# A concatenated kernel of dilated attention and a state-space scan: projections reordered, logits partly summed on TensorE, states stacked, and three engines in a written order

## The chip, the cores and the metric

The kernel runs on one core of one Trainium2 chip. A core has a matrix engine (PE, TensorE), a vector engine (DVE), a scalar engine (ACT), GpSimd (POOL) and a queue engine (SP) that issues DMAs. The metric is the device time of one execution in microseconds; lower is better. A trace by the hardware profiler accompanies it.

## The reference

Two independent parts read the same kind of input and are concatenated along the last axis. S = 2048 positions, D = 448 features, bf16 in and out.

```python
# A: sliding dilated attention, 16 heads of 28, window of 8 positions 2 apart
qkv = x @ wqkv                       # split into q, k, v per head
idx = pos[:, None] - 2 * arange(8)   # earlier positions only, masked where negative
logits = einsum("bhsd,bhswd->bhsw", q, k[idx]) * 28 ** -0.5
o = einsum("bhsw,bhswd->bhsd", softmax(logits), v[idx])
a = o @ wo
# B: diagonal complex state space, P = 448 states
Lam_bar = exp(exp(log_dt) * Lam);  B_bar = ((Lam_bar - 1) / Lam)[:, None] * Bmat
h_t = Lam_bar * h_{t-1} + B_bar @ x_t           # over 2048 steps
y = 2 * real(h @ Cmat.T) + x * Dskip
return concatenate([a, y], -1)
```

## The kernel before

**Part A.** A partition holds 16 consecutive positions (J = 16). `g_xta` transposes x on PE, four blocks of 128x112 into one PSUM tile, and DVE copies that to `xTA`. `proj(t, ...)` (L144 matmuls, L146 ACT copies) then computes v, k and q, in this order, sixteen positions of four matmuls of 448 columns each. The 14 positions before a partition's first one, the halo, come from the partition below: four DMAs on SP per tensor (L149 to L152) copy them inside SBUF. The one of L151 starts at partition 112, which the one of L150 writes too; the one of L152 fills a lone row. For each of the 8 offsets w DVE multiplies q by the shifted k (L327, `pr`, 7168 elements per partition), then adds halves (L329, L330) and, for two offsets together, the rest of a tree (L331 to L333) to give the logits `L`. Softmax runs on DVE with one Exp on ACT (L341). Then DVE multiplies the weights by v (L380, `pv`), PE sums over the 8 offsets and transposes at once by matmuls with the identity into `acc` (L385), ACT copies `acc` to `oT` (L387), and `wo_group` multiplies by wo (L367) and stores `ya`.

**Part B.** Time is cut into 512 chunks of T = 4 steps. x is transposed on PE (`g_x4`, L116) into `xT4`; B likewise (`g_bt`, L110, copied by ACT at L111) and C (`g_ct`, L122). The 448 states have a real and an imaginary tile of 112 rows for each of four `pt`: eight tiles. For each step j, Bu takes four matmuls (L256), and from j = 1 two more with diagonal matrices `dg` that carry the state of the step before (L260, L261). `ssm_chunk_scan` on DVE rotates by the tables `tab` (cos, sin), scans over the 512 chunks (L278) and rotates back, for each half of the tiles. A fix (L294 to L296) adds the chunk's incoming state to steps 0 to 2, and `c_side` (L306, L308) multiplies by C and the skip term and stores `yo`. Parameters (powers of Lam_bar, `dg`, C's weights `Cw`, the tables) are computed on DVE and ACT from four vectors of 448 numbers.

**What sets the order.** The program is written in the order v, small parameters, k, Cw, q, B's transposes, Bu, scans, fix, C, logits, softmax, output. A list scheduler of the framework reorders each engine's instructions; semaphores keep the dependences. Each engine runs its own list in order. A DMA is issued by the engine on whose queue it stands (SP, ACT or POOL), which waits there for what the DMA needs; DMA semaphores are reused in turn, so that an issue can also wait for an earlier DMA that used the same one.

Of the kernel before, what the change touches and what calls it, by code (L numbers as in the profile page):

```python
# [8 lines left out]
BF16 = mybir.dt.bfloat16  # L9
# [10 lines left out]
T = 4  # L20
NC = S // T
# [6 lines left out]
def kernel(  # L28
# [21 lines left out]
    const = ctx.enter_context(tc.tile_pool(name="const", bufs=1))  # L50
    psum = ctx.enter_context(tc.tile_pool(name="ps", bufs=4, space=bass.MemoryType.PSUM))
    pst_ctx = ExitStack()
    psum_t = pst_ctx.enter_context(tc.tile_pool(name="pst", bufs=2, space=bass.MemoryType.PSUM))
    ident = const.tile([128, 128], BF16, tag="ident")
    make_identity(nc, ident[:])

    bk = ctx.enter_context(tc.tile_pool(name="b_keep", bufs=1, side="right"))
    bx = ctx.enter_context(tc.tile_pool(name="b_x", bufs=1, side="right"))
    bn_ctx = ExitStack()
    bn = bn_ctx.enter_context(tc.tile_pool(name="b_n", bufs=1, side="right"))  # L60
    ak = ctx.enter_context(tc.tile_pool(name="a_keep", bufs=1))
    qk_ctx = ExitStack()
    qkp = qk_ctx.enter_context(tc.tile_pool(name="a_qk", bufs=1))
    ain_ctx = ExitStack()
    ain = ain_ctx.enter_context(tc.tile_pool(name="a_in", bufs=1))

    def rows112(src):
        return src.rearrange("(k p) n -> p k n", p=KT)
    xnA = ain.tile([128, J, D], BF16, tag="xnA")
    xA_r = A_x[0].rearrange("(p j) d -> p j d", j=J)  # L70
    nc.sync.dma_start(xnA[:, 0:4, :], xA_r[:, 0:4, :])
    nc.sync.dma_start(xnA[:, 4:8, :], xA_r[:, 4:8, :])
    nc.sync.dma_start(xnA[:, 8:12, :], xA_r[:, 8:12, :])
    nc.sync.dma_start(xnA[:, 12:16, :], xA_r[:, 12:16, :])
    wq = ain.tile([KT, 4, 3 * D], BF16, tag="wqkv")
    nc.sync.dma_start(wq[:, 0:2], rows112(A_wqkv)[:, 0:2])
    nc.sync.dma_start(wq[:, 2:4], rows112(A_wqkv)[:, 2:4])

    raws = []
    for i, (vec, name) in enumerate(((B_Lambda_re, "lre"), (B_Lambda_im, "lim"), (B_log_dt, "ld"), (B_Dskip, "dsk"))):  # L80
        raw = const.tile([KT, 4], BF16, tag=name + "_raw", name=name + "_raw")
        nc.sync.dma_start(raw[:], vec.rearrange("(t i) -> i t", i=KT))
        raws.append(raw)
    Cn = bn.tile([KT, 2, 4, D], BF16, tag="Cn")
    nc.sync.dma_start(Cn[:, 0], rows112(B_C_re))
    nc.gpsimd.dma_start(Cn[:, 1], rows112(B_C_im))
    Bn = bn.tile([KT, 2, 4, D], BF16, tag="Bn")
    nc.sync.dma_start(Bn[:, 0], rows112(B_B_re))
    nc.gpsimd.dma_start(Bn[:, 1], rows112(B_B_im))
    xnB = bx.tile([128, 4, T, D], BF16, tag="xnB")  # L90
    xB_r = B_x[0].rearrange("(cb p j) d -> p cb j d", p=128, j=T)
    nc.sync.dma_start(xnB[:, 0:2], xB_r[:, 0:2])
    nc.gpsimd.dma_start(xnB[:, 2:4], xB_r[:, 2:4])

    xTA = ain.tile([KT, 4, J, 128], BF16, tag="xTA")
    CT = bn.tile([KT, 4, 2, D], BF16, tag="CT")
    BT = bk.tile([KT, 4, 2 * D], BF16, tag="BT")
    xT4 = bk.tile([KT, 4, T, NC], BF16, tag="xT4")
    idk = ident[0:KT, 0:KT]

    def g_xta(jg, kt):
        tp = psum_t.tile([128, 4, 128], BF16, tag="tp", name="tp")
        for jj in range(4):
            PE.transpose(tp[0:KT, jj, :], xnA[:, 4 * jg + jj, KT * kt:KT * (kt + 1)], ident[:])  # L104
        V.tensor_copy(xTA[:, kt, 4 * jg:4 * jg + 4, :], tp[0:KT])  # L105

    def g_bt(ri, kt):
        tp = psum_t.tile([128, 4, 128], BF16, tag="tp", name="tp")
        for pt in range(4):
            PE.transpose(tp[0:KT, pt, 0:KT], Bn[:, ri, pt, KT * kt:KT * (kt + 1)], idk)  # L110
        ACT.copy(BT[:, kt, ri * D:(ri + 1) * D].rearrange("p (a b) -> p a b", a=4), tp[0:KT, :, 0:KT])  # L111

    def g_x4(kt, j):
        tp = psum_t.tile([128, 4, 128], BF16, tag="tp", name="tp")
        for cb in range(4):
            PE.transpose(tp[0:KT, cb, :], xnB[:, cb, j, KT * kt:KT * (kt + 1)], ident[:])  # L116
        ACT.copy(xT4[:, kt, j, :], tp[0:KT])

    def g_ct(ri, pt):
        tp = psum_t.tile([128, 4, 128], BF16, tag="tp", name="tp")  # L120
        for dtile in range(4):
            PE.transpose(tp[0:KT, dtile, 0:KT], Cn[:, ri, dtile, KT * pt:KT * (pt + 1)], idk)  # L122
        V.tensor_copy(CT[:, pt, ri, :].rearrange("p (a b) -> p a b", a=4), tp[0:KT, :, 0:KT])

    groups = ([(g_xta, (jg, kt)) for jg in range(4) for kt in range(4)]
              + [(g_ct, (ri, pt)) for ri in range(2) for pt in range(4)]
              + [(g_bt, (ri, kt)) for ri in range(2) for kt in range(4)]
              + [(g_x4, (kt, j)) for j in range(T) for kt in range(4)])

    def next_group(n=1, late=False):  # L130
        for _ in range(n):
            if groups and (late or groups[0][0] in (g_xta, g_ct)):
                fn, args = groups.pop(0)
                fn(*args)
    next_group(4)

    q_s = qkp.tile([128, DH, J, H], BF16, tag="q_s")
    k_s = qkp.tile([128, JK, DH, H], BF16, tag="k_s")
    v_s = ak.tile([128, JK, DH, H], BF16, tag="v_s")
    def proj(t, dst, joff):  # L140
        for j in range(J):
            ps = psum.tile([128, 512], F32, tag="mm")
            for kt in range(4):
                PE.matmul(ps[:, 0:D], xTA[:, kt, j, :], wq[:, kt, t * D:(t + 1) * D], start=(kt == 0), stop=(kt == 3))  # L144
            o_ap = dst[:, :, j, :] if t == 0 else dst[:, joff + j, :, :]
            ACT.copy(o_ap, ps[:, 0:D].rearrange("p (h d) -> p d h", h=H))  # L146
            next_group()
        if t != 0:
            nc.sync.dma_start(dst[1:65, 0:HALO], dst[0:64, J:JK])  # L149
            nc.sync.dma_start(dst[65:113, 0:HALO], dst[64:112, J:JK])  # L150
            nc.sync.dma_start(dst[112:128, 0:HALO], dst[111:127, J:JK])  # L151
            nc.sync.dma_start(dst[0:1, 0:HALO], dst[0:1, J:JK])  # L152

    proj(2, v_s, HALO)
    def pt_(name):
        return const.tile([KT, 4], F32, tag=name, name=name)
    lre, lim, ld, dsk = [pt_(n) for n in ("lre", "lim", "ld", "dsk")]
    for f_, r_ in zip((lre, lim, ld, dsk), raws):
        V.tensor_copy(f_[:], r_[:])
    hpib = const.tile([KT, 1], F32, tag="hpib")  # L160
    nc.gpsimd.memset(hpib[:], 0.5 * PI * SHR)
# [9 lines left out]
    def sincos(sin_out, cos_out, y, kM, pool, shape, tagp):  # L171
        nfr = pool.tile(shape, F32, tag=tagp + "nfr", name=tagp + "nfr")
        V.scalar_tensor_tensor(nfr[:], kM, -MAGIC, y, ALU.add, ALU.subtract)
        ACT.activation(sin_out, nfr[:], ACTF.Sin, scale=-2 * PI * SHR)
        afr = pool.tile(shape, F32, tag=tagp + "afr", name=tagp + "afr")
        ACT.activation(afr[:], nfr[:], ACTF.Abs)
        ACT.activation(cos_out, afr[:], ACTF.Sin, bias=hpib[:], scale=-2 * PI * SHR)

    dt = pt_("dt"); ACT.activation(dt[:], ld[:], ACTF.Exp)
    are = tt(pt_("are"), dt, lre, ALU.mult)  # L180
    th = tt(pt_("th"), dt, lim, ALU.mult)
    r = pt_("r"); ACT.activation(r[:], are[:], ACTF.Exp)
    rT = pt_("rT"); ACT.activation(rT[:], are[:], ACTF.Exp, scale=float(T))
    f = ts(pt_("f"), th, 1.0 / (2 * PI), ALU.mult)
    fT = ts(pt_("fT"), th, float(T) / (2 * PI), ALU.mult)
    kM1 = pt_("kM1"); V.tensor_scalar(kM1[:], f[:], 1.0, MAGIC, ALU.mult, ALU.add)
    sn = pt_("sn"); cs = pt_("cs")
    sincos(sn[:], cs[:], f[:], kM1[:], const, [KT, 4], "p_")
    pwall = const.tile([KT, T - 1, 3, 4], F32, tag="pwall")
    a1 = tt(pwall[:, 0, 0, :], r, cs, ALU.mult)  # L190
    b1 = tt(pwall[:, 0, 1, :], r, sn, ALU.mult)
    pw = [(a1, b1)]
    t0 = pt_("t0"); t1 = pt_("t1")
    for k in range(2, T):
        ap, bp = pw[-1]
        ak_ = pwall[:, k - 1, 0, :]; bk_ = pwall[:, k - 1, 1, :]
        tt(ak_, ap, a1, ALU.mult); tt(t0, bp, b1, ALU.mult); tt(ak_, ak_, t0, ALU.subtract)
        tt(bk_, ap, b1, ALU.mult); tt(t0, bp, a1, ALU.mult); tt(bk_, bk_, t0, ALU.add)
        pw.append((ak_, bk_))
# [25 lines left out]

    proj(1, k_s, HALO)
    Cw = bk.tile([KT, 8, D], BF16, tag="Cw")
    dgD = bk.tile([KT, 4, KT], BF16, tag="dgD")
    for pt in range(4):
        c1 = slice(pt, pt + 1)  # L230
        tmp = bn.tile([KT, D], F32, tag="ctmp")
# [189 lines left out]
```

## Time and profile before

| | |
|---|---|
| median of 3 runs | 231.79 us (231.47 to 232.53) |
| span of the profiled execution | 227.3 us, 3441 instructions; 4.5 us less than the median |
| PE, weight loads | 181.1 us (80%), 118.0 us (52%) |
| DVE | 161.9 us (71%) |
| ACT | 105.1 us (46%) |
| mean granted TensorE clock | 0.946 |
| read from HBM, written | 6.88 MB, 3.67 MB |

The time of the profiled execution itself is not listed beside its span, so the difference between median and span, 4.5 us, is taken for what lies around the span. Busy times are of one profiled execution. An engine's slices are 40 equal parts of the span, each digit the busy share in tenths. The chain of waits is the work that ended last, followed back from the end at each step to what released it. A group's line reads: line of the kernel, engine, operation, out<-in, shapes, count | busy us, mean ns of one | idle time before them and what ended most of it. Matmuls are pipelined, so the mean of one is longer than the distance from one start to the next.

### The profile page before, as it was taken

To read this page: it belongs to the slowest core of one execution; us is meant where nothing else is said; L and a number is where in the kernel's file an instruction comes from. 1 tells how busy PE (TensorE), PEld (TensorE's weight loads), DVE (VectorE), ACT (ScalarE), POOL (GpSimd) and SP (SyncE) were. 2 spreads that over 40 slices of the span, in tenths; PEclk is the share of its full clock that TensorE was granted. 3 is DMA by queue.
4 is the path that set the end of the run, shared out by engine and by line. 5 is a ranking of instruction groups with operands and counts; after the bars stand their busy time and mean duration, and the time that the engine had idled before them with its cause. 6 is when DMAs were issued, how large, how long until landed. Compare 5 with 4: busy or idle time off the path is not lost.

```text
span 227.3 us, 3441 instructions
## 1 busy us (share of the span) xinstructions
PE 181.1 (80%) x1400; PEld 118.0 (52%) x1400; DVE 161.9 (71%) x200; ACT 105.1 (46%) x186; POOL 4.8 (2%) x18
## 2 busy tenths in 40 slices
PE   2008995989997999999969400599999996999993
PEld 2004662645555666566536200255555696887961
DVE  1103779794007999179999999999867999999022
ACT  2001691898678876454438300293345213234151
POOL 6000000000000000000000000000000000000000
PEclk9999999799999799999999955599999999999999
DMA  6999300392752000000000000001112230020213
GB/s 227 283 291 204 136 4 0 71 178 40 141 108 35 3 0 0 3 0 0 0 0 0 3 0 0 0 0 40 62 43 81 62 114 3 0 84 3 82 36 128
DMA packets 9996, 14.02 MB, mean 62 GB/s; under 512 B 2716, under 2 KB 8188, under 8 KB 9724
## 3 DMA queue, kind: packets, MB, share of 16 engines
q1 hardware_dynamic: 9612, 12.07, 21.2%
q0 software_dynamic: 368, 1.72, 2.6%
q8 instruction: 11, 0.18, 0.3%
q14 instruction: 5, 0.04, 0.1%
HBM read 6.88 MB, written 3.67 MB: 46 GB/s over the span
## 4 chain that ended last, share of the span: by engine, by line
PE 57%; DVE 25%; ACT 8%; DMA 7%; SPq 1%; issue 1%
PE acc L385 13%; PE ps L144 12%; PE ps L306 11%; DMA wq<-in_A_wqkv_dram 7%; PE psf L256 6%; PE ps L367 5%; DVE pr L327 5%; DVE scr L278 4%; DVE pr L329 3%; DVE dg L212 2%; PE tp L116 2%; PE psf L295 2%; PE psf L296 1%; PE ps L308 1%; PE psf L261 1%; PE psf L260 1%
## 5 line engine op out<-in xcount | busy, mean ns | idle before, releaser
L144 PE MATMUL ps<-wq,xTA 112*128 112x448 bf16 x192 | 44.9, 376 | 15.6 <-DMA wq<-in_A_wqkv_dram 11.9
L327 DVE TENSOR_TENSOR pr<-q_s,k_s 128x7168 bf16<-128x7168 bf16 x8 | 31.1, 3885 | 15.9 <-ACT q_s L146 15.9
L256 PE MATMUL psf<-xT_115,BT 112*112 112x512 bf16 x128 | 33.7, 386 | 0.0
L380 DVE TENSOR_TENSOR pv<-attn,v_s 128x1792 bf16<-128x1792 bf16 x32 | 32.2, 1082 | 0.0
L385 PE MATMUL acc<-ident,pv 128*112 128x128 bf16 x512 | 29.2, 219 | 2.0 <-ACT oT L387 2.0
L385 PEld LDWEIGHTS <-pv 128*112 128x112 bf16 x512 | 29.0, 130 | 2.3 <-issue 2.0
L144 PEld LDWEIGHTS <-xTA 112*128 112x128 bf16 x192 | 18.9, 103 | 20.3 <-issue 4.3
L306 PE MATMUL ps<-Cw,Z 112*128 112x448 bf16 x128 | 26.8, 352 | 0.0
L262 ACT CAST Z<-psf 112x512 bf16<-112x512 f32 x32 | 18.8, 587 | 16.9 <-PE psf L261 15.5
L295 PE MATMUL psf<-Z,dg 112*112 112x511 bf16 x24 | 10.1, 419 | 18.8 <-DVE Z L282 18.8
L297 ACT CAST Z<-psf 112x512 bf16<-112x512 f32 x24 | 14.0, 585 | 22.9 <-PE psf L296 21.7
L256 PEld LDWEIGHTS <-BT 112*112 112x112 bf16 x128 | 16.7, 132 | 9.9
L146 ACT CAST v_s<-ps 128x448 bf16<-128x448 f32 x16 | 8.3, 538 | 26.8 <-PE ps L144 26.7
L105 DVE COPY xTA<-tp 112x512 bf16<-112x512 bf16 x16 | 6.7, 422 | 19.6 <-PE tp L104 19.4
L387 ACT CAST oT<-acc 112x2048 bf16<-112x2048 f32 x4 | 7.5, 1865 | 22.8 <-PE acc L385 22.8
L310 ACT CAST yo<-ps 128x448 bf16<-128x448 f32 x16 | 8.3, 531 | 17.9 <-DMA out_dram<-yo 9.8
L104 PEld LDWEIGHTS <-xnA 128*112 128x112 bf16 x64 | 7.3, 164 | 18.0 <-issue 12.5
L306 PEld LDWEIGHTS <-Z 112*128 112x128 bf16 x128 | 11.8, 98 | 9.0
L329 DVE TENSOR_TENSOR pr<-pr 128x3584 bf16<-128x3584 bf16 x8 | 16.1, 2016 | 0.1
L296 PEld LDWEIGHTS <-dg 112*112 112x112 bf16 x24 | 3.4, 142 | 21.5 <-issue 19.9
L367 PE MATMUL ps<-wo_p,oT 112*128 112x448 bf16 x64 | 12.6, 352 | 0.0
L104 PE MATMUL tp<-ident,xnA 128*112 128x128 bf16 x64 | 7.7, 259 | 4.4 <-DMA xnA<-in_A_x_dram 4.3
(131 smaller groups left out, 234.3 us busy)
## 6 DMA issues: line engine op xcount, KB each, us to landing
xnA<-in_A_x_dram SPq DMA_DIRECT2D x4, 448.0 KB, 6.8
out_dram<-yo SPq DMA_DIRECT2D x16, 112.0 KB, 1.7
out_dram<-ya SPq DMA_DIRECT2D x16, 112.0 KB, 1.7
wq<-in_A_wqkv_dram SPq DMA_DIRECT2D x2, 588.0 KB
xnB<-in_B_x_dram POOLq DMA_DIRECT2D x1, 896.0 KB, 13.2
xnB<-in_B_x_dram SPq DMA_DIRECT2D x1, 896.0 KB
v_s<-v_s SPq DMA_DIRECT2D x1, 784.0 KB
k_s<-k_s SPq DMA_DIRECT2D x1, 784.0 KB
```

The costliest lines, as they stand in the source:

```text
L104: PE.transpose(tp[0:KT, jj, :], xnA[:, 4 * jg + jj, KT * kt:KT * (kt + 1)], ident[:])
L144: PE.matmul(ps[:, 0:D], xTA[:, kt, j, :], wq[:, kt, t * D:(t + 1) * D], start=(kt == 0), stop=(kt == 3))
L256: PE.matmul(ps[:], BT[:, kt, ri * D + KT * pt: ri * D + KT * (pt + 1)], xT4[:, kt, j, :], start=(kt == 0), stop=(kt == 3 and j == 0))
L262: ACT.copy(Z[:, ri * 4 + pt, j, :], ps[:])
L295: PE.matmul(ps[:, 1:NC], dg[:, pt, j, ia, :], Z[:, pt, T - 1, 0:NC - 1], start=False, stop=False)
L297: ACT.copy(Z[:, ri * 4 + pt, j, :], ps[:])
L306: PE.matmul(ps[:, 0:D], Z[:, k8, j, cols], Cw[:, k8, :], start=(k8 == 0), stop=False)
L327: V.tensor_tensor(pr.rearrange("p d (j h) -> p d j h", h=H), q_s[:], k_s[:, off:off + J].rearrange("p j d h -> p d j h"), ALU.mult)
L329: V.tensor_tensor(pr[:, 0:14, :], pr[:, 0:14, :], pr[:, 14:28, :], ALU.add)
L367: PE.matmul(ps[:, 0:D], oT[:, kt, j, :], wo_p[:, kt, :], start=(kt == 0), stop=(kt == 3))
L380: V.tensor_tensor(pv[:], attn[:, w, JG * H * jg:JG * H * (jg + 1)].rearrange("p (j h) -> p j h", h=H) .unsqueeze(2).to_broadcast((128, JG, ...
L385: PE.matmul(acc[0:KT, kt, jj, :], pvf[:, jj, KT * kt:KT * (kt + 1)], ident[:], start=(w == 0 and jj == 0), stop=(w == W - 1 and jj == JG - 1))
```

## The change

- **Order of part A.** The projections are now k, q, v. x is loaded in four pieces with k's weights second; weights are loaded per projection. k's halo DMAs are issued from ACT, v's from SP.
- **Logits.** Each offset is cut in two halves of 8 positions. DVE multiplies and adds the two halves of the head dimension once; PE sums the remaining 14 terms in PSUM by matmuls with the identity; ACT copies the result to `L`.
- **States.** Seven tiles of 128 rows, each 64 real rows above the same 64 imaginary ones. One matrix `R` of 128x128 per tile and power carries the complex product, in place of two diagonal ones. The scan's rotation reads rows 0 to 63 and writes rows 64 to 127, and the reverse.
- **B's x** is transposed by eight DMAs on SP, straight to `xT4`. B's and C's loads move from POOL to SP. The vectors come in twelve small DMAs on POOL into 33 rows, ahead of the identity on POOL, and are transposed on PE. Tables are computed once in natural order and spread to the stacked order by twelve DMAs on SP. C is interleaved by POOL.
- **Written order.** From v's projection on, PE, DVE and ACT run in the order in which the program emits them. `fill(us)` takes pieces of PE work from a list until their written cost reaches the given time; `qk_unit` places such a piece between the DVE work of a unit and its matmuls. After unit 12 the list holds three pieces, so the loop `while len(work) > 12` takes none; the scans of both halves follow unit 12, and units 13 to 15 come after them.

```diff
+    for hj in range(2):
+        xh = qkp.tile([128, 8, D], BF16, tag="prod", bufs=3, name="xh")
+        nc.sync.dma_start(xh[:, 0:4], xA_r[:, 8 * hj:8 * hj + 4])
+        if hj == 0:
+            load_w(1)
+        nc.sync.dma_start(xh[:, 4:8], xA_r[:, 8 * hj + 4:8 * hj + 8])
+    load_w(0)
...
+    for j in range(T):
+        nc.sync.dma_start_transpose(xT4[:, 0:3, j, :], xB_r[j, :, 0:384])
+        nc.sync.dma_start_transpose(xT4[:, 3, j, :], xB_r[j, :, 320:448])
+    rows = const.tile([33, 128], BF16, tag="rows")
+    for r0, vec in ((0, B_Lambda_re), (7, B_Lambda_im), (18, B_log_dt)):
+        for hf in range(2):
+            nc.gpsimd.dma_start(rows[r0:r0 + 7, 64 * hf:64 * hf + 64], vec.rearrange("(m i) -> m i", i=64))
...
     ident = const.tile([128, 128], BF16, tag="ident")
     make_identity(nc, ident[:])
...
+    for jg in range(4):
+        for kt in range(4):
+            g_xta(jg, kt)
+        for j in range(4 * jg, 4 * jg + 4):
+            proj_j(1, k_s, HALO, j)
+    halo(nc.scalar, k_s)
...
+    for j in range(J):
+        proj_j(0, q_s, 0, j)
+    ctx.enter_context(tc.manual_schedule(engines={nc.tensor.engine, nc.vector.engine, nc.scalar.engine}))
...
+    def qk_unit(u, us):
...
+        V.tensor_tensor(pr.rearrange("p d (j h) -> p d j h", h=H), q_s[:, :, 8 * jh:8 * jh + 8, :],
+                        k_s[:, off + 8 * jh:off + 8 * jh + 8].rearrange("p j d h -> p d j h"), ALU.mult)
+        V.tensor_tensor(pr[:, 0:14, :], pr[:, 0:14, :], pr[:, 14:28, :], ALU.add)
+        fill(us)
+        for d in range(14):
+            PE.matmul(lgs[g][:, wi, 128 * jh:128 * jh + 128], ident[:], pr[:, d, :], start=(d == 0), stop=(d == 13))
+        if u % 4 == 3:
+            ACT.copy(L[:, 2 * g:2 * g + 2, :], lgs[g][:])
...
+    for u in range(13):
+        qk_unit(u, 2.3)
+    while len(work) > 12:
+        fill(0.1)
+    ssm_chunk_scan(HF[0])
+    fill(99)
+    ssm_chunk_scan(HF[1])
+    for ms in HF:
+        for j in range(T - 1):
+            for m in ms:
+                work.append((0.43, fix_tile, (m, j)))
+    for j in [T - 1] + list(range(T - 1)):
         for ct in range(4):
+            work.append((1.55, c_tile, (j, ct)))
+    for u in range(13, 16):
+        qk_unit(u, 3.6 if u == 13 else 2.3)
...
+            if w % 2 == 1 and w < W - 1:
+                fill(0.7)
         ACT.copy(oT[:, :, JG * jg:JG * (jg + 1), :], acc[0:KT])
+        fill(2.0)
+        for j in range(JG * jg, JG * (jg + 1)):
+            work.append((0.76, wo_tile, (j,)))
```

## The prediction

> **What bounds the kernel now.** I read the slices of the page first, then the chain of waits in order of time, then the groups, then the timeline of the two DMA-issuing queues. The slices (5.7 us each) show who is full when:
>
> ```profile
> PE   2008995989997999999969400599999996999993
> DVE  1103779794007999179999999999867999999022
> PEclk9999999799999799999999955599999999999999
> ```
>
> PE has nothing from slice 3 to the start of slice 4 and a hole around slices 22 to 26; DVE is nearly empty in slices 10 to 12, while q is projected, and full from 17 to 30. The chain says the same with names; its columns are start, duration, what:
>
> ```profile
> 3.19 16.09 DMA wq<-in_A_wqkv_dram
> ...
> 50.01 19.09 PE ps L144 x100
> ...
> 119.58 3.80 DVE pr L327
> ...
> 180.88 7.16 PE acc L385 x128
> ```
>
> So four stretches set the end: loads until 19.3; projections on PE until 69.1 (DVE's first product waits 15.9 us for q_s); products and scan on DVE until 144.8; then PE to the end. The last execution spans 227.3 us; the median of the runs is 231.79, so 4.5 us lie around the span. I sum against 227.3 and add 4.5.
>
> **What the change removes.** The groups (busy, mean ns) price the products:
>
> ```profile
> L327 DVE TENSOR_TENSOR pr<-q_s,k_s 128x7168 bf16<-128x7168 bf16 x8 | 31.1, 3885 | 15.9 <-ACT q_s L146 15.9
> L329 DVE TENSOR_TENSOR pr<-pr 128x3584 bf16<-128x3584 bf16 x8 | 16.1, 2016 | 0.1
> ```
>
> Per offset w, DVE does 3.80 + 1.94 + 1.0 us start to start, and per two offsets 0.87 + 0.60 + 0.60 more: 8 x 6.74 + 4 x 2.07 = 62 us. After, two half units per w cost 1.93 + 1.0 each: 16 x 2.93 = 47 us. DVE loses 15 us. PE gains 224 small matmuls; 128 like them (L385) take 7.16 us, 0.056 each, so 0.78 per unit, 12.5 in all. Seven stacked tiles in place of eight: Bu 28 tiles of 4 or 5 matmuls at 0.216 (29 us, was 37), fix 21 x 2 x 0.216 (9, was 15), C 16 x (7 x 0.189 + 0.2) = 16 x 1.52 (24, was 27). The 64 PE transposes of B's x go (64 x 0.056 = 4 warm, and 16 ACT copies, 8.8 us). Scan: eight operations per half, 64-row ones priced like L271 (1.14 start to start, 112 rows; half the rows could be cheaper or, across rows, dearer; I take equal), 8 x 1.14 + 4 x 1.12 = 13.6, then 8 x 0.87 + 3 x 1.12 = 10.3; 23.9, as before. The matrix R is 2688 of dg's 4032 columns, 2.9 for 4.36; four L copies of 0.59 come to ACT. PE's total falls by about 11 us, DVE's by 15. What is left is decided by the waits.
>
> **Start.** x comes in order of use, and wk second, so the 16.09 us wait for wq shrinks to about 5 us. But the order of POOL's instructions now has twelve row DMAs ahead of the identity, for which the first transpose waits. The timeline of POOL and SP in the run before (start, duration, engine, line):
>
> ```profile
> 2.52 0.71 POOL L89 DMA_DIRECT2D Bn<-in_B_B_im_dram  x1
> 3.23 0.73 POOL L93 DMA_DIRECT2D xnB<-in_B_x_dram  x1
> ...
> 57.57 0.51 SPq L149 DMA_DIRECT2D k_s<-k_s  x1
> 58.13 0.59 SPq L150 DMA_DIRECT2D k_s<-k_s  x1
> 58.77 2.64 SPq L152 DMA_DIRECT2D k_s<-k_s  x1
> 67.30 0.53 SPq L151 DMA_DIRECT2D k_s<-k_s  x1
> ```
>
> 0.71 and 0.73 for very different shapes: I take 0.73 whatever the size, 0.75 + 12 x 0.73 = 9.5, with memset, iota and select (0.2 + 0.58 + 0.3) 10.7. Small DMAs might cost less, to nothing at best. Then four rounds of 16 transposes and 16 matmuls for k. A warm round is 15 matmuls at 0.19 plus a serial head of transposes and copies through two buffers (about 1.9): 4.8. The first is cold (four matmuls and four transposes took 1.92 at 20 to 25 us, 0.98 later): 7.9. k ends at 10.7 + 7.9 + 14.4 = 33.0, and ACT's last k copy at 33.7.
>
> **The halo of k moves from SP to ACT.** This is where the new wait sits. ACT is in order, and L136 to L139 stand in it after dt. The rows above: issues of 0.51, 0.59 and 2.64, then the fourth waits until L150's transfer has landed (both write row 112), 67.30 - 57.57 = 9.7 us after the first. On SP nobody stood behind; on ACT r, the table of Sin, all q_s copies and the sincos tables do. PE fills its four banks of q and stops. Issue from 33.8, ACT free at 33.8 + 9.8 + 0.5 = 44.1. [...]
>
> **q, tables, Cw.** Start to start on ACT before: a copy 0.45, one sincos of 512 columns 2.3 (0.53 + 0.52 + 0.61 + 0.61), table load 1.28. The written order up to the eighth q_s copy: 2.7 of small ones, then 8 copies, 4 sincos and 2 ctmp: 2.7 + 3.6 + 9.2 + 1.0 = 16.5, so DVE's first unit starts at 60.6, only 9 us before today's 69.7. Then Cw 2 to 6 stand between the units on DVE, each needing an ACT ctmp and PE transposes into the two buffers that the Cw before must free: 1.93 + 0.6 + 1.0 + 0.6 + 1.4 + 0.6 + 1.9 + 0.6 + 0.9 = 9.5, to 70.1. Logits of unit 0 end at 71.0.
>
> **Units.** PE sets the pace, since three product buffers tie DVE to it: units 1 to 3, 4 x 0.76 + 0.78 = 3.84 each, 82.5; unit 4 with seven BT copies on ACT 5.2, 87.7; unit 5 3.4; units 6 to 9 4.0 each, 107.1. DVE's unit 12 waits for that: 110.0. Scans to 133.9, units 13 to 15 to 142.7. PE has only three Bu and nine fix tiles meanwhile and idles some 8 us. What such a hole costs, in the windows (span, busy of five engines, clock):
>
> ```profile
> 140.00:144.80 4.80, 0.00 (x1) 0.00 (x1) 4.80 (x6) 0.00 (x0) 0.00 (x0) 0.50 0.00 0
> 144.80:148.10 3.30, 3.29 (x8) 1.57 (x8) 3.30 (x3) 1.49 (x3) 0.00 (x0) 0.51 0.00 0
> 148.10:153.50 5.40, 5.40 (x27) 3.19 (x25) 5.33 (x5) 4.90 (x9) 0.37 (x2) 1.00 0.00 0
> ```
>
> After the hole PE runs 3.3 us at half clock, 1.7 lost. From 136.8: logits 1.5, six fix tiles 3.7, 0.8, six at ACT's 0.5 3.0, 0.8: 146.6; copy and POOL's memset 1.2: softmax starts at 147.8.
>
> **Softmax to end.** Maximum and subtraction 4.7 (163.54 to 168.28 today): 152.5. Exp now stands behind four yo copies on ACT: PE 146.6 + 4 x 1.52 + 0.7 = 153.4, table and Exp 3.2, 156.6, about 1 us later than DVE needs. Sums to attn 6.55: 163.1; first pv 164.2. PE then has acc 4 x 7.16 = 28.6, eight C tiles 12.2, sixteen wo tiles 12.1, two waits on oT copies (1.87 each, partly covered) 1.9, cold start 1.7: 220.7. Last copy 0.8 and the final store 2.9 (224.4 to 227.3 today): **224.4, with 4.5 around it 228.9 us**; I say 229.
>
> **Transposes by DMA** take no term: 2.10 MB, no row of the kind. At the load rate of 4.28 to 16.86 us (299 GB/s) 7 us; at the rate of a yo store (112 KB in 1.7 us, 67 GB/s) 31. I take near 10, since these too are loads to all rows. They start when 4.6 MB are in, at 17, and xT4 is wanted at 87. But ACT's halo issues reuse semaphores of the first four transposes, so those must land by 33.8: 1.05 MB in 16.8 us, 62 GB/s. [...]
>
> Behind them on SP stand the twelve table DMAs (1.84 MB, at the halo's 201 GB/s 9 us); nat is ready at 59, so they land by 70. The first L copy waits for them, since L takes nat's place, at 83: hidden, with 13 us to spare. The halo of v follows, wanted at 164, and the loads of B and C, moved from POOL to SP, are wanted after 33: both free.
>
> **Rivals.**
> 1. Cheap start: small row DMAs cost little, the identity is there at 5.5 when wk lands, everything moves up by 5.2: 223.7. For it: three descriptors are few; against: 0.71 and 0.73 at different sizes. Chance 0.2.
> 2. PE stays full from 71.0: v 12.2, BT 1.6, logits 12.5, Bu 28.7, fix 9.1, C 24.3, acc 28.6, wo 12.1, less the first unit's 3.8, are 125.3 us, to 196.3; with the tail of 3.7 and 4.5 around it 204.5. Against it: DVE's 24 us of scan with no PE work written beside it. 0.06.
> 3. Slower: the DMA transposes run at 62 GB/s or less, so ACT stands at the halo until the fourth lands, and the halo shares the rings with the other four (up to 1.05 MB, 16 us more). Each us that ACT is freed after 44.1 is a us at the end; from 4 us on the kernel is slower than before. At 8 to 16 us late 237 to 245; I take 241. For it: strided pieces; against: 299 GB/s for loads. 0.17.
> The forecast case has 0.57, spread 222 to 236 by the bounds of the start, the halo and the cold clock.
>
> **Numbers.** 0.5% of 231.79 is 1.2 us, about what a measurement here can tell. Faster: 0.2 + 0.06 + 0.57 x 0.55 = 0.57; same 0.57 x 0.19 = 0.11; slower 0.17 + 0.57 x 0.26 = 0.32. Range 217 to 241, which leaves out rival 2 and the slow half of rival 3; the likeliest case alone is 222 to 236.
>
> **What would show it.** Right: first PE transpose near 10.7, k copies done near 34, a gap of some 10 us on ACT before r whose releaser is the halo DMA, q copies between 47 and 66, DVE units at 3.8 to 4 us paced by PE, a PE hole beside the scans at half clock, pv from 163. Wrong: PE starting near 5 (rival 1), no ACT gap, PE without holes after 71 (rival 2), or ACT waiting past 45 on a transpose's semaphore (rival 3).

## The result and the profile after

| | before | after |
|---|---|---|
| median, same chip, 20 executions each | 231.84 us (229.16 to 233.03) | 232.99 us (231.82 to 236.30) |
| ratio after / before | | 1.0069, 95% interval 1.0043 to 1.0095 |
| span of the profiled execution | 227.3 us | 231.5 us (its own time 233.44) |
| busy PE, DVE, ACT | 181.1, 161.9, 105.1 us | 183.3, 143.7, 99.4 us |
| mean granted TensorE clock | 0.946 | 0.947 |

The changed kernel is slower by 0.7%: 233.0 us where 229 was forecast, against 231.8 before. The range held it, the sign was wrong. The medians here and below are of all executions, while a ratio compares only the fast ones of both kernels, so it is not always the quotient of two medians. DVE lost 18 us of work where 15 were forecast, and PE, which was to lose 11, gained 2. The slices of the page (5.8 us each):

```profile
PE   0198990276999979999999506999479999999973
DVE  0024330498799968657999999471999836486002
PEclk9999999579999999999999965999979999999999
```

Counted from 1, the hole of PE in slices 7 and 8 is ACT standing at k's halo. The one in slices 23 and 24 lies beside the scans, and the lowered clock begins in it and outlasts it (slices 24 and 25, 0.6 and 0.5). From slice 11 to slice 22 PE is nearly full. Against before, DVE's full stretch has moved to the middle and has gaps wherever PE sets the pace.

The steps of the forecast, read from the timelines of PE, DVE and ACT (us from the span's start):

| | forecast | after |
|---|---|---|
| first PE transpose; last k copy done | 10.7; 33.7 | 10.57; 31.3 |
| ACT past the halo | 44.1 | 41.75 |
| DVE's unit 0 starts; its logits end | 60.6; 71.0 | 58.20; 69.34 |
| logits of unit 9 end | 107.1 | 108.87 |
| scans start; end | 110.0; 133.9 | 112.09; 138.05 |
| softmax starts; Exp's result used; weights ready | 147.8; 156.6; 163.1 | 152.09; 161.76; 168.29 |
| first pv matmul; PE ends; span | 164.2; 220.7; 224.4 | 169.54; 227.95; 231.5 |

In distances: 1.7 us early at unit 0's logits; then +3.4 up to unit 9, +0.3 to the scans, +2.1 in the scans, +0.1 to softmax, +0.9 to Exp, +1.9 from the first pv to PE's end, and the rest below 0.2 each: 7 us late at the end.

**The halo on ACT, as forecast.** The timeline of ACT and of its DMA issues (start, duration, engine, line; in brackets the idle time and what ended it):

```profile
31.32 0.56 ACTq L136 DMA_DIRECT2D k_s<-k_s  x1
31.92 0.60 ACTq L137 DMA_DIRECT2D k_s<-k_s  x1
32.55 2.66 ACTq L139 DMA_DIRECT2D k_s<-k_s  x1
41.16 0.54 ACTq L138 DMA_DIRECT2D k_s<-k_s  x1
41.75 0.21 ACT L175 ACTIVATE r<-are 128x7 f32<-128x7 f32 x1 [10.35 <-DMA k_s<-k_s]
```

The four issues cost what they cost on SP before (0.51, 0.59, 2.64 and 0.53), the last waits for L137's landing 9.2 us after its issue, and the first parameter operation behind them stands 10.35 us (forecast 9.8 and 0.5).

**Bu's tiles, not as forecast.** A tile of one step was to take 0.86 us (j = 0) or 1.08. The weight loads of one tile, from the timeline of PE's weight loads (in brackets the time in which no weights were loaded, called a stand below):

```profile
112.65 0.37 PEld L292 LDWEIGHTS <-BT 128*128 128x128 bf16 x3
113.45 0.09 PEld L292 LDWEIGHTS <-BT 64*128 64x128 bf16 x1 [0.42 <-issue]
113.77 0.10 PEld L295 LDWEIGHTS <-R 128*128 128x128 bf16 x1 [0.23 <-issue]
113.78 0.53 PEld L292 LDWEIGHTS <-BT 128*128 128x128 bf16 x3
```

The fourth block of features is 64 rows, which lie in partitions 64 to 127. Its weights are loaded only after a stand of 0.42 us, those of `R` behind it after another 0.23, and the tile takes 1.29 us start to start (112.71, 114.00, 115.28 in PE's timeline). C's tiles have the same block in their skip term. Two tiles of C in the kernel before, where all blocks have 112 rows, and two after it:

```profile
153.36 1.68 PE L306 MATMUL ps<-Cw,Z 112*128 112x448 bf16 x8
...
155.07 1.68 PE L306 MATMUL ps<-Cw,Z 112*128 112x448 bf16 x8
```

```profile
152.41 1.50 PE L352 MATMUL mm<-Cw,Z 128*128 128x448 bf16 x7
153.75 0.46 PE L356 MATMUL mm<-dgD,xT 128*128 128x128 bf16 x4
154.14 1.50 PE L352 MATMUL mm<-Cw,Z 128*128 128x448 bf16 x7
```

1.73 us from tile to tile where 1.52 was taken: with seven matmuls in place of eight the tile costs more than the 1.71 of before. The load of the 64 rows takes 0.09 us and that of 128 rows 0.10, so the loads themselves do not make the tile dearer. Whether the stands of 0.42 and 0.23 come from the block's height of 64 or from its start at row 64 was not separated.

**The scans.** DVE's timeline at their start:

```profile
112.09 1.22 DVE L326 TENSOR_TENSOR scr<-Z,tab 64x2048 bf16<-64x2048 bf16 x1
113.32 1.22 DVE L327 TENSOR_TENSOR scr<-Z,tab 64x2048 bf16<-64x2048 bf16 x1
114.58 1.22 DVE L328 TENSOR_TENSOR Z<-Z,tab 128x2048 bf16<-128x2048 bf16 x1
```

1.23 to 1.26 from start to start, where 1.14 was taken from the kernel before. There the operations are as long, but operations of part A stand between them, and the next one starts before the end of the last:

```profile
126.38 1.21 DVE L272 TENSOR_TENSOR Z<-Z,tab 112x2048 bf16<-112x2048 bf16 x1
127.52 1.08 DVE L330 TENSOR_TENSOR l_1534<-pr 128x1792 bf16<-128x1792 bf16 x1
```

The hole that the scans leave PE, in the windows (span, busy of PE, weight loads, DVE, ACT and POOL, clock, share and rate of DMA):

```profile
126.10:141.16 15.06, 3.98 (x18) 1.66 (x17) 14.74 (x15) 5.06 (x10) 0.00 (x0) 0.80 0.00 0
141.16:145.40 4.24, 4.24 (x21) 2.47 (x21) 4.21 (x3) 1.17 (x2) 0.00 (x0) 0.51 0.00 0
```

PE has 4 us of work in 15, then 4.2 us at half clock.

**The transposes by DMA** were issued from 11.77 to 29.25 and the first four, whose landings the trace gives, landed 4.0 to 9.7 us after their issue: hidden, long before xT4 is wanted at 84. Some 20 us for all eight (to about 33, an estimate that gives the last the 4 to 5 us of the second to fourth) lies in the forecast's bounds (7 to 31), above the 10 taken.

### The profile page after: what moved, and what is told of

Same layout as the page of the kernel before. It is cut to its first block, busy times and chain, and to the rows that moved or that the text cites. A ratio compares the mean times of both kernels' runs of the same rounds, so it can differ in the third digit from the quotient of the medians.

```text
span 231.5 us, 3653 instructions
## 1 busy us (share of the span) xinstructions
PE 183.3 (79%) x1487; PEld 110.0 (47%) x1492; DVE 143.7 (62%) x174; ACT 99.4 (43%) x175; POOL 16.9 (7%) x41
## 4 chain that ended last, share of the span: by engine, by line
PE 68%; DVE 14%; ACT 7%; DMA 6%; issue 2%; POOL 1%; ACTq 0%; DVEq 0%; POOLq 0%
PE acc L433 14%; PE mm L131 13%; PE mm L292 12%; PE mm L352 8%; PE lg L318 6%; PE mm L415 4%; DMA k_s<-k_s 4%; PE mm L295 3%; DMA rows<-in_B_Lambda_re_dram 2%; PE mm L356 2%; PE tp L125 2%; ACT oT L437 2%; DVE scr L331 1%; PE mm L341 1%; PE mm L342 1%
## 5 line engine op out<-in xcount | busy, mean ns | idle before, releaser
L131 PE MATMUL mm<-xw 112*128 112x448 bf16 x192 | 44.7, 377 | 11.8 <-ACT q_s L133 11.8
L428 DVE TENSOR_TENSOR pv<-attn,v_s 128x1792 bf16<-128x1792 bf16 x32 | 33.0, 1086 | 11.2 <-PE acc L433 11.1
L313 DVE TENSOR_TENSOR prod<-q_s,k_s 128x3584 bf16<-128x3584 bf16 x16 | 32.3, 2021 | 9.3 <-PE lg L318 9.0
L131 PEld LDWEIGHTS <-xw 112*128 112x128 bf16 x192 | 18.2, 103 | 30.2 <-issue 16.3
L292 PE MATMUL mm<-xT,BT 128*128 128x512 bf16 (+1 forms) x107 | 30.9, 381 | 0.4
L296 ACT CAST Z<-mm 128x512 bf16<-128x512 f32 x28 | 16.4, 586 | 23.6 <-PE mm L295 18.9
L318 PE MATMUL lg<-prod,ident 128*128 128x128 bf16 x224 | 15.9, 225 | 10.6 <-DVE prod L315 10.6
L352 PE MATMUL mm<-Cw,Z 128*128 128x448 bf16 x112 | 23.9, 353 | 0.0
L318 PEld LDWEIGHTS <-ident 128*128 128x128 bf16 x224 | 14.2, 101 | 13.6 <-issue 11.6
L315 DVE TENSOR_TENSOR prod<-prod 128x1792 bf16<-128x1792 bf16 x16 | 17.4, 1090 | 0.5
L343 ACT CAST Z<-mm 128x512 bf16<-128x512 f32 x21 | 10.8, 614 | 13.6 <-PE mm L342 13.6
L415 PE MATMUL mm<-wo_p,oT 112*128 112x448 bf16 x64 | 13.8, 352 | 1.2 <-ACT oT L437 1.2
L420 ACT CAST ya<-mm 128x448 bf16<-128x448 f32 x14 | 7.2, 537 | 13.3 <-PE mm L415 10.7
L125 PEld LDWEIGHTS <-xh 128*112 128x112 bf16 x64 | 5.8, 149 | 12.5 <-issue 7.3
```

What stands on the lines that cost most here:

```text
L125: PE.transpose(tp[0:KT, jj, :], xnA[jg // 2][:, 4 * (jg % 2) + jj, KT * kt:KT * (kt + 1)], ident[:])
L131: PE.matmul(ps[:, 0:D], xTA[:, kt, j, :], wq[:, t, kt, :], start=(kt == 0), stop=(kt == 3))
L292: PE.matmul(ps[:], BT[blk_rows(blk), blk, m, :], xT4[blk_rows(blk), blk, j, :], start=(blk == 0), stop=(blk == 3 and j == 0))
L296: ACT.copy(Z[:, m, j, :], ps[:])
L313: V.tensor_tensor(pr.rearrange("p d (j h) -> p d j h", h=H), q_s[:, :, 8 * jh:8 * jh + 8, :], k_s[:, off + 8 * jh:off + 8 * jh + 8].rearra ...
L315: V.tensor_tensor(pr[:, 0:14, :], pr[:, 0:14, :], pr[:, 14:28, :], ALU.add)
```

## The experiments

Theory at the start: the two tile prices (A) turned the sign, the halo on ACT (H) is what costs most, and PE's start waits for the row DMAs. The first four runs take one of these each. All were timed against the kernel before on the same chip; the first logits end between 68.7 and 71.2 in different executions of kernels that are the same up to there, so distances within a run compare better than its marks.

### Full 128-row blocks in Bu and C

```diff
-    Bn = bk.tile([128, NM, D], BF16, tag="scr", name="Bn")
+    Bn = bk.tile([128, NM, 512], BF16, tag="scr", name="Bn")
...
-            PE.matmul(ps[:], BT[blk_rows(blk), blk, m, :], xT4[blk_rows(blk), blk, j, :],
+            PE.matmul(ps[:], BT[:, blk, m, :], xT4[:, blk, j, :],
...
-            PE.matmul(ps[:, f0:f0 + rw.stop - rw.start], xT4[rw, blk, j, cols], dgD[rw, blk, rw],
+            PE.matmul(ps[:, f0:f0 + rw.stop - rw.start], xT4[:, blk, j, cols], dgD[:, blk, rw],
```

`Bn`'s columns 384 to 447 are set to zero on POOL and features 384 to 447 loaded to columns 448 to 511, so the weights of the 64 added rows are zeros. B is loaded by four DMAs in place of two for this.

> The fourth feature block of Bu and of C's skip term uses all 128 rows (64 of them zero weights) in place of rows 64 to 127; the numbers of matmuls and columns stay. Theory A (a matmul on rows 64 to 127 costs about 0.1 us where it comes in and 0.1 where it goes out, since its weight load is not hidden): a Bu tile with R goes from 1.29 to 1.08 us, a C tile from 1.73 to 1.52, a unit with three Bu tiles from 4.65 to 4.0; unit 12 ends 3.2 us earlier, four C tiles ahead of Exp give 0.8, the eight in the pv stage 1.7: span 231.5 - 5.7 = 225.8. Rival B (the longer tiles come from the stacked matrix R, from 128-column weights or from the engine's pace after logits): tiles unchanged, span 231.5.

Measured: 228.72 us, ratio 0.9986 (0.9919 to 1.0053), span 226.5. A second and longer comparison of the same kernel:

> The full-row kernel once more, timed in five rounds, since its first comparison could not tell it from the kernel before. If the two tile prices are what turned the sign, 5.3 to 5.9 us leave the changed kernel's span of 231.5 less what the start scatters by, and the ratio to the kernel before goes from 1.007 to about 0.985; if the traces' tile times are given back elsewhere it stays at 1.00 or above.

Measured: 228.56 us, ratio 0.9925 (0.9873 to 0.9977), span 226.6. The timeline of the weight loads of the first of the two runs, and its tiles of C:

```profile
113.81 0.59 PEld L294 LDWEIGHTS <-BT 128*128 128x128 bf16 x4
114.51 0.10 PEld L297 LDWEIGHTS <-R 128*128 128x128 bf16 x1
```

```profile
151.08 1.49 PE L354 MATMUL mm<-Cw,Z 128*128 128x448 bf16 x7
152.40 0.36 PE L358 MATMUL mm<-dgD,xT 128*128 128x128 bf16 x4
152.60 1.49 PE L354 MATMUL mm<-Cw,Z 128*128 128x448 bf16 x7
```

The stands are gone. A tile of Bu takes 1.08 and a tile of C 1.52, to the hundredth the forecast's prices. Unit 0's to unit 9's logits take 36.19 us in both runs, where the changed kernel took 39.53 and the forecast had 36.1. The stage from the first pv to PE's end is 56.66 and 56.79 for 58.41 (forecast 56.5). With more rows computed, and besides only B's loads and a memset on POOL altered, the kernel is on the other side of the kernel before: the first interval still holds 1.00, the second does not. The second expectation's 0.985 was too low, outside the interval like 1.00. One saving did not come. From the maximum to the use of Exp's result the two runs take 9.26 and 9.48 us for 9.67, not 0.8 less: Exp stands behind the fourth copy of a C tile on ACT, and that copy waits for the store of the first one to give its buffer free, since `yo` has three. In the first run it starts 2.1 us after the copy before it, the others 1.52.

### Full rows in C alone

The third pair of lines of the diff above.

> Only C's skip matmul uses all 128 rows; Bu stays as in the changed kernel. Theory A: C tile 1.73 to 1.52, Bu tile stays 1.29; 4 x 0.21 ahead of Exp and 8 x 0.21 in the pv stage, span 229.0. Rival B: no change. Together with the run of both it says how much Bu alone is worth (3.2 by A).

Measured: 232.10 us, ratio 0.9974 (0.9931 to 1.0018), span 230.9. C's tiles are at 1.52, the last stage at 56.71 and unit 0 to unit 9 still at 39.54, so each price is undone by its own edit. The span does not show it: this execution's first logits end at 71.22, 1.9 us later than in the changed kernel's. Span alone is inconclusive here; the distances are not.

### The halo of k on SP

```diff
-    halo(nc.scalar, k_s)
+    halo(nc.sync, k_s)
```

> k's halo is issued on SP, as before, not on ACT; all else as changed. Theory H (ACT stands 10.35 us at the fourth issue and everything behind it moves): r starts near 31.5, not 41.75, unit 0's logits end near 59.5, and since PE sets the pace after that, the whole moves: span 221.5 to 222.5. Rival: the wait is taken back later (tables behind the halo on SP, or PE's q stage becomes the bound), span 227 or more.

Measured: 224.66 us, ratio 0.9715 (0.9671 to 0.9758), span 222.5. ACT's timeline:

```profile
30.56 0.21 ACT L175 ACTIVATE r<-are 128x7 f32<-128x7 f32 x1 [0.30 <-DVE are L159]
```

r starts 11.2 us earlier, the first logits end 10.3 earlier, the span is 9.0 shorter, as theory H has it; 0.8 is given back between scans and softmax, 0.4 in the last stage. On SP the four issues stand from 30.17 to 40.79 as they did on ACT, behind the transposes, and nobody waits for them. One line thus carries more than the whole loss. On ACT the issues and their wait are 10.35 us with work behind them, and choosing SP wins 9.0.

### Is it the wait or the issues?

```diff
-        eng.dma_start(dst[112:128, 0:HALO], dst[111:127, J:JK])
+        eng.dma_start(dst[113:128, 0:HALO], dst[112:127, J:JK])
```

> The four halo DMAs of k stay on ScalarE; the third now writes partitions 113 to 127 instead of 112 to 127 (partition 112 is written by the second with the same values), so no issue has to wait for another one's landing. Theory W (the wait for the landing is the price, the issues themselves little): what stays on ScalarE is 0.56 + 0.60 + 2.66 + 0.54 = 4.4 us, r at 31.2 + 4.4 = 35.7 instead of 41.75, and the span 231.5 - 6 = 225.5. Rival Q (any issue on this engine stops it until the queue takes it, since the rings still carry the transposes): r stays near 41 and the span near 231.5.

Measured: 229.21 us, ratio 0.9985 (0.9928 to 1.0042), span 229.0.

```profile
32.82 3.17 ACTq L138 DMA_DIRECT2D k_s<-k_s  x1
36.03 2.38 ACTq L139 DMA_DIRECT2D k_s<-k_s  x1
38.45 0.21 ACT L175 ACTIVATE r<-are 128x7 f32<-128x7 f32 x1 [6.78 <-issue]
```

Neither theory as written. Without the overlap nothing waits for a landing, but the issues alone now hold ACT 6.8 us, since the third took 3.17 and not 0.54. Of 10.35, the overlap cost some 3.6, and 6.8 is left for issuing. Why an issue of fifteen rows takes 3.17 behind the others and one of sixteen rows 0.54 after their landing was not settled.

### The identity first

```diff
+    ident = const.tile([128, 128], BF16, tag="ident")
+    make_identity(nc, ident[:])
     rows = const.tile([33, 128], BF16, tag="rows")
```

> The identity is built on POOL ahead of the twelve row DMAs. First PE transpose near 4.7 (when x's first piece lands), not 10.57: 5.9 us earlier if x and k's weights keep pace, k's last copy near 25.5. Theory: 5 to 5.9 us come through to the end, span 226. Rival: the halo of k, now issued near 25.5, meets the DMA transposes that run until 32 and takes longer than 9.2 us, so that only 2 to 3 come through: span 229.

Measured: 232.47 us, ratio 1.0015 (0.9970 to 1.0060), span 229.3. ACT behind the halo, and the last two transposes on SP:

```profile
38.84 0.21 ACT L175 ACTIVATE r<-are 128x7 f32<-128x7 f32 x1 [14.18 <-DMA k_s<-k_s]
```

```profile
27.18 6.26 SPq L91 DMA_TRANSPOSE xT<-in_B_x_dram  x1
33.48 3.74 SPq L92 DMA_TRANSPOSE xT<-in_B_x_dram  x1
```

PE starts at 4.62 and the copies of k end 6.7 earlier, but the halo now runs among the transposes: its second DMA lands 13.0 us after issue in place of 9.2, the last transposes' issues take 6.26 and 3.74 where they took 2.25 and 1.26, and ACT stands 14.18 us. Of 6.7 won, 2.9 reach r and 2.2 the end. The rival held. The forecast's rival 1 (cheap start, 5.2 us) would thus have paid less than half, for a reason that its text did not have.

### Units 13 to 15 between the scans

```diff
     ssm_chunk_scan(HF[0])
     fill(99)
+    for j in range(T - 1):
+        for m in HF[0]:
+            work.append((0.43, fix_tile, (m, j)))
+    for u in range(13, 16):
+        qk_unit(u, 1.6)
     ssm_chunk_scan(HF[1])
...
+    fill(9 * 0.43 - 0.1)
...
-    fill(5.0)
     ACT.activation(L[:], L[:], ACTF.Exp, scale=float(DH) ** -0.5)
...
-    fill(6.0)
+    fill(9.2)
```

> Units 13 to 15 stand between the two scans instead of after both, each with four fix tiles of the first half as its filler; the nine fix tiles of the second half follow the second scan, Exp stands directly behind them, and six multiplications by C follow Exp. Theory M (what VectorE has to do up to the maximum is the bound there): scan 126.7, units to 135.9, second scan to 147.2, so the maximum starts at 147.2 instead of 152.1 and the weights are ready at 162 instead of 168.3. Ten tiles of C instead of eight are then left for the last stage, 3.5 us more, so PE ends at 225.2 instead of 227.95 and the span is 228.7. Rival P (PE has the same sum to do after its hole, and the hole only moves): the span stays at 231.5 within 1.

Measured: 228.88 us, ratio 0.9998 (0.9953 to 1.0043), span 226.4. The maximum starts at 146.52, the weights are ready at 163.04, and the last stage, with two more tiles of C in it, takes 58.59 us for 58.41. The windows of that stage, of this run and of the changed kernel:

```profile
164.29:222.88 58.59, 58.58 (x686) 44.78 (x686) 32.34 (x32) 19.36 (x28) 0.00 (x0) 1.00 0.15 48
```

```profile
169.54:227.95 58.41, 56.77 (x664) 44.20 (x664) 32.44 (x32) 18.48 (x26) 0.00 (x0) 0.97 0.13 43
```

PE came to the last stage after 1.66 us without work and not after 4.95, and its clock is 1.00 there and not 0.97; the 1.6 us in which it idled within the stage are gone too; that pays for most of the 3.5 us of two tiles. M held in its direction, with 5.1 us of span gained for 2.8 expected (0.6 of it is this execution's earlier start, so 4.5 from the first logits to the end). The hole did not go: PE has no work for 10.22 us before the second half's first fix tile. The ratios, 0.9998 here and 1.0069 for the changed kernel, put the gain at some 1.6 us only; its size is thus open, the distances within the run are not.

### Weaving the second scan

```diff
+    g1 = scan_steps(HF[1])               # ssm_chunk_scan as a generator, one operation a step
+    next(g1)
     for u in range(13, 16):
-        qk_unit(u, 1.6)
-    ssm_chunk_scan(HF[1])
+        qk_unit(u, 1.6, lambda: next(g1))  # one step after the product, one after the sum
+    for _ in g1:
+        pass
```

> As the run with units 13 to 15 between the scans, but VectorE's six operations of these units are woven one by one between the first seven operations of the second scan. Theory S (an operation that reads what the one before it wrote starts only after that one's end, 0.03 to 0.04 us after it, while an independent neighbour starts 0.08 us before it): twelve of the stretch's joints become independent, some 0.1 us each, so from the first scan's end to the second scan's end 20.57 becomes 19.4, and the span 226.4 becomes 225.3. Rival (the distance is a property of the operations, 64-row and 128-row ones simply cost 1.24 where 112-row ones cost 1.14): the stretch stays at 20.5.

Measured: 228.52 us, ratio 0.9888 (0.9823 to 0.9952), span 227.2 (its first logits end 1.1 later than in the run above). From the first scan's end to the second's it takes 20.05 us: 0.5 less, where theory S counted 1.2. From the first logits to the end only 0.3 us are gone (157.4 for 157.7), which a span cannot tell from its scatter.

```profile
127.12 0.95 DVE L328 TENSOR_TENSOR scr<-Z,tab 64x1536 bf16<-64x1536 bf16 x1
128.11 2.03 DVE L313 TENSOR_TENSOR prod<-q_s,k_s 128x3584 bf16<-128x3584 bf16 x1
...
132.16 0.95 DVE L332 TENSOR_TENSOR Z<-Z,tab 128x1536 bf16<-128x1536 bf16 x1
133.02 2.02 DVE L313 TENSOR_TENSOR prod<-q_s,k_s 128x3584 bf16<-128x3584 bf16 x1
```

The rival falls: the same rotation step of 0.95 is followed after 0.86 by an independent product at 133.02, where in the unwoven scan it was followed after 0.98 to 1.0. Two things were missed in the count. Four of the joints, the places where one operation ends and the next starts (sum to next product, scan to scan), overlapped before the weaving too: 1.01 us from start to start for a sum of 1.09, and three scans in 3.46 where one alone takes 1.22. And three do not overlap although independent: those at 128.11, 130.16 and 131.15, which start 0.99, 2.05 and 0.99 after the start of operations of 0.95, 2.03 and 0.95, all next to the two operations that read or write from row 64 on. The joint between L326 and L327 in the changed kernel, 1.23 for an operation of 1.22, is of the same kind. No run here varied the rows alone, so that the rows are the cause was not shown.

### The edits together

> Full 128-row blocks in Bu and C together with the halo of k on SyncE. If the two causes are separate they add: from the span of the halo alone, 222.5, the 3.3 us of Bu's tiles and the 2.2 us of the last stage go: 217.0. Rival: Bu's saving is lost, because the tables, the rotation matrix or the states are late once everything starts 10 us earlier: 219 or more.

Measured: 219.75 us, ratio 0.9600 (0.9524 to 0.9675), span 217.7: unit 0 to unit 9 take 36.19 us, and the two causes add to within 0.7 of the span that was expected. The last stage is 58.13 us and not the 56.6 of the full rows alone: it ran at a mean clock of 0.95 and not 0.97.

> As the run with the three edits, and the identity is built ahead of the twelve row DMAs on GpSimd. With the halo off ScalarE nothing there stands behind the transposes by DMA: the first PE transpose starts at 4.6 instead of 10, the copies of k end at 24.5, and everything up to the end moves up by 5: span 212. Rival: the halo, on SyncE behind eight transposes whose issues last until 29 to 37, lands at 50 and k is late for the units that need it (they start near 43 then): 215 to 217.

Measured: 213.48 us, ratio 0.9335 (0.9259 to 0.9412), span 211.7. PE starts at 4.76, r at 25.40, unit 0 at 42.69: r is 6.2 us earlier than in the run above, where the identity alone had brought it 2.9 forward: what was lost at the halo is there once nobody on ACT waits for it. On SP the halo's last issue still stands until 40.10, and no unit was late for it.

> All five edits: full rows in Bu and C, k's halo on SyncE, identity first, units 13 to 15 between the scans. If the last edit is worth here what it was alone (the start of the maximum 4.9 us earlier relative to the first scan, 4.5 us at the end): from 211.7 to a span of 207.2. Rival: PE, now the fuller engine in the last two stages, gives half of it back: 209.5 or more.

Measured: 209.59 us, ratio 0.9051 (0.9010 to 0.9093), span 208.0, 0.8 above what was expected and below the rival's 209.5; its first logits end 0.9 later than in the run above.

> The five edits and the woven second scan: 1.1 us less than the five edits if theory S of the weaving holds and the stretch is on the path, so about 206; the same as the five edits, 207.2, if not.

Measured: 208.32 us, ratio 0.9009 (0.8972 to 0.9046), span 205.5: 10% faster than the kernel before. From the first logits to the end it is 152.7 us for 153.2, so the weaving is worth some 0.6 here; the other 1.9 of the 2.5 between the two spans are an earlier start of this execution.

## Why the prediction was wrong, point by point

- **Start, halo, first units: right in kind, 1.7 us too dear.** 0.73 per row DMA was 0.51, but some of them waited for earlier ones (the chain has 5.49 us of a rows DMA), so PE starts where forecast; k's rounds were 2.3 shorter, and unit 0 took 0.7 longer. Rivals 1 (PE from 5 on) and 3 (ACT past 45) did not come: 10.57 and 41.75. The halo, the largest single term, was priced from SP's rows at 9.8 and 0.5 and measured 10.35; without the wait for a landing the issues alone took 6.8.
- **The step that failed: "Bu 28 tiles of 4 or 5 matmuls at 0.216" and "C 16 x (7 x 0.189 + 0.2)".** The first counts every matmul at the price of one in a stream of equal heights. The fourth block has 64 rows, and changing to it and back costs 0.21 us per tile: 1.29 for 1.08, 1.73 for 1.52. In units 4 to 9, 16 tiles of Bu make it the +3.4, in the last stage it is 8 x 0.21 = 1.7 of the +1.9. Of the +0.9 before Exp the full rows took back only 0.2 to 0.4; the rest fits the wait for a buffer of `yo`, which the forecast did not have. The full-row runs show the two prices: 36.19 us for the forecast's 36.1 in units 1 to 9, 56.7 for 56.5 in the last stage, and a ratio of 0.9925. The forecast had PE lose 11 us, though the terms that it lists (8, 6, 3 and 4 less 12.5) add up to some 8.5; 44 tiles of Bu and C at 0.21 give 9.2 back.
- **The second term: scans at 23.9, measured 26.0.** 1.14 start to start came from operations with independent neighbours. Written one behind the other, each starts only when the one before has ended, after 1.23 to 1.26. The weaving run shows it for part of the joints: 0.86 to an independent product after the same step of 0.95 that was 0.98 to 1.0 before.
- **The base.** "4.5 us lie around the span" was wrong: in 20 executions of the changed kernel it is 1.92 to 2.01, and in those of the kernel before that were timed beside the experiments 1.72 to 1.84. The profiled execution of before, at 227.3, was then one of its faster ones, some 229.1 us where the median was 231.8. With 2.0 around it the forecast span of 224.4 is 226.4 us, 2.3% under before; the two mis-sized terms, some 5.3 and 2.1 us, took all of that and more. The span missed by 7.1; the wrong base hid 2.5 of it, which is luck, so that the time missed by 4 only.
- **Hole and cold clock: right.** 13.9 us from the scans' end to softmax was forecast, 14.0 measured, with the half clock where it was put (4.24 us of it, 3.3 forecast). Agreement to 0.1 is partly luck: in the runs that keep this order the stretch takes 13.3 to 14.9.
- **Transposes by DMA: right to be free, the rival's mechanism real but elsewhere.** They did not delay ACT here; in the identity run ACT stood longer, 14.18 us for 10.35, where the halo met them.
- **Rival 2** (PE full after 71) is refuted by slices 23 and 24.
- **Slips that cost nothing.** In the slices of the kernel before, PE has nothing in slices 2 and 3, counted from 1, not from 3 to the start of 4; no term uses it. The sum of 11 us for PE is no term of the time either.

## What to carry to other kernels

A matmul's price read from a stream of equal heights need not hold where the heights change: here a block in rows 64 to 127 among full ones cost 0.21 us a tile more than the same block filled up with zeros, so padding is worth a trial. DMA issues belong on an engine with nothing behind them, and above all those that wait for another DMA's landing: here they held ACT 10.35 us, and moving them to SP was worth 9.0 of the span. A price taken start to start belongs to its neighbours (1.14 us for a rotation step among independent operations, 1.23 to 1.26 without them): when a change takes independent work from between dependent operations, price them end to end, and read the time around the span from more than one execution before leaning a small difference on it.

## What the runs showed of the hardware that was not expected

- No weights are loaded for 0.42 us before those of a block in rows 64 to 127 and for 0.23 before the next full one; the tile takes 0.21 us longer than with four full blocks (1.29 for 1.08).
- Issuing four DMAs held ACT 6.8 us even where none had to wait for another's landing (0.55, 0.60, 3.17 and 2.38).
- In the run in which the halo was issued among the DMA transposes both were slower: 13.0 us for a halo transfer that took 9.2, and issues of 6.26 and 3.74 for 2.25 and 1.26.
- In the timelines shown here a DVE operation starts about 0.1 us before the end of an independent neighbour (0.86 from start to start for a step of 0.95, 1.01 for a sum of 1.09). A dependent one starts after that end (0.99 to 1.0 for 0.95), and so did independent ones next to an operation that reads or writes from row 64 on (0.98 and 0.99 for 0.95, 1.23 for 1.22).
